# Loading Wk in two pieces and splitting each transposed-tile copy between VectorE and ScalarE at the start of a gated attention-and-MLP kernel

## The chip, the cores and the metric

The kernel runs on one core of a Trainium2 chip. Its time is the device time of one execution in microseconds (us), as the median of several executions. A core has a matrix engine (TensorE, called PE in the profile; PEld is its weight load), a vector engine (VectorE, DVE), an activation engine (ScalarE, ACT), a general engine (GpSimd, POOL) and a queue engine (SyncE, SP). SP, ACT and POOL can issue DMA transfers; what they issue stands in the profile as SPq, ACTq and POOLq. Each engine works through its own list of instructions in order, and waits for others through semaphores.

## The reference

The input x is 2048 rows (tokens) of 512 numbers in bf16. Two blocks work on the same x and are mixed with a gate per row:

```
g   = sigmoid(sum(x * gate_w))                   # one number per row
A:  q, k, v = split(x @ wqkv)                    # 32 heads of 16
    phi(t) = where(t > 0, t + 1, exp(t)) + 1e-6
    kv  = phi(k)^T v per head;  z = sum over rows of phi(k)
    a   = (phi(q) kv) / (phi(q) z + 1e-6) @ wo
B:  h   = layernorm(x);  u = gelu(h^T w1 + b1)   # over the rows: 2048 -> 1792
    b   = (u w2 + b2)^T                          # back to 2048 rows
out = g * a + (1 - g) * b
```

## The kernel before

Rows are cut into 16 tiles of 128 (`NT`), the 512 columns into 4 chunks of 128 (`ND`). The work is written out in one order, and each engine keeps the order in which its own instructions were written. The matrix engine goes through these stages:

1. Six products of constants (`wps`, line 113, called at L201), which need no input.
2. The head: x tiles 0, 1 and 2 are transposed by products with an identity matrix (`pt`), one PSUM bank per tile, and the bank is copied to `xT` in SBUF: by VectorE (L212) for tiles 0 and 2, by ScalarE (L210) for tile 1. Then `k_part` forms K = x Wk for these three tiles (`kacc`, 4 products of 128x128 by 128x512 per tile, one for each chunk of Wk), chunk 0 of all tiles first, then chunk 1, then chunks 2 and 3 tile by tile.
3. A loop over tiles 3 to 15. The transposed x of these tiles comes by transposing DMA loads from SP (L135), the first of which brings tiles 3 and 4. Each turn forms K of tile t, then adds the product of tile t-4 of x and of phi(K) to `gacc` (`g_tile`, which collects x^T phi(K) in four banks). After the loop follow `g_tile` 12 to 15.
4. Q and the first MLP product together (`qacc`, `uacc`), the rest of `uacc`, small products for kv, and last per row tile `aps` and `yps`, mixed by VectorE at L505 and stored.

`phi` of a tile is one exponential on ScalarE (L216) and two operations on VectorE (L217, L220), which write `pk`. VectorE also takes layer-norm statistics (`ln_step`: L240 and L241 per tile). In the head `ln_step(0)` and `ln_step(1)` come before the three `k_phi`; in the loop `ln_step(t - 3)` comes after `k_phi(t)` from t = 5.

At the start SP and ACT issue 7 loads of 128 KB: SP x tile 0 and Wk chunks 0 and 2, ACT x tiles 1 and 2 and Wk chunks 1 and 3. The first transposing load waits for a small VectorE copy (L160) that itself waits for x tile 0. Later SP issues the rest of x, Wq, and w1 in chunks of up to 4 blocks; the first w1 chunk in two transfers, the others in one.

Of the kernel before, what the change touches and what calls it, by code (L numbers as in the profile page):

```python
# [7 lines left out]
ACT = mybir.ActivationFunctionType  # L8
# [7 lines left out]
def kernel(  # L16
# [13 lines left out]
    nc = tc.nc  # L30
# [7 lines left out]
    S, D = X.shape  # L38
    F = B_w1.shape[1]
    NT = S // P  # L40
    ND = D // P
# [13 lines left out]
    wqkv_view = A_wqkv.rearrange("(k p) n -> p k n", p=P)  # L55
# [11 lines left out]
    def keep(shape, dtype, name):  # L67
        return persist.tile(shape, dtype, name=name, tag=name)

    def bank(name, dtype=FP32):  # L70
        return ps.tile([P, SC], dtype, name=name, tag="bank")
# [5 lines left out]
    wk_sb = keep([P, ND, D], BF16, "wk_sb")  # L77
# [34 lines left out]
    def mm(o, lhsT, rhs, start, stop, **kw):  # L112
        nc.tensor.matmul(o, lhsT=lhsT, rhs=rhs, start=start, stop=stop, **kw)  # L113
# [14 lines left out]
    def load_x(q, t0, n):  # L128
        q.dma_start(out=xs[:, t0 : t0 + n, :], in_=x_view[:, t0 : t0 + n, :])

    def load_wk(q, k):
        q.dma_start(out=wk_sb[:, k, :], in_=wqkv_view[:, k, D : 2 * D])

    def load_xT(t0, n):
        nc.sync.dma_start(  # L135
# [1 line left out]
        )  # L137

    load_x(nc.sync, 0, 1)
    load_x(nc.scalar, 1, 1)  # L140
    load_wk(nc.sync, 0)
    load_x(nc.scalar, 2, 1)
    for k, q in ((1, nc.scalar), (2, nc.sync), (3, nc.scalar)):
        load_wk(q, k)
    nc.vector.memset(ones_f[:], 1.0)
    nc.vector.memset(mhalf[:], -0.5)
    nc.vector.memset(Z32[:], 0.0)
# [2 lines left out]
        out=ident[:], in_=ident[:], compare_op=ALU.not_equal, fill=1.0, base=0,  # L150
# [5 lines left out]
        out=maskQ[:], in_=maskH[:].rearrange("p (a m) -> p m a", m=2), op=ALU.max, axis=AX.X  # L156
# [4 lines left out]
        out=xT[:, :, 3 * P : 3 * P + 2],  # L161
        in_=xs[:, 0, 0 : 2 * ND].rearrange("p (k c) -> p k c", k=ND),
# [10 lines left out]
    for c, (j0, nb) in enumerate(w1_chunks):  # L173
        w = wpool.tile([P, NT, FB * P], BF16, name="w1c", tag="wc")
        w1c.append(w)
        for t0 in range(0, NT, 8) if c == 0 else (0,):
            t1 = t0 + 8 if c == 0 else NT
            nc.sync.dma_start(
                out=w[:, t0:t1, : nb * P], in_=w1_view[:, t0:t1, j0 * P : (j0 + nb) * P]
            )  # L180
        if c == 0:
            nc.sync.dma_start(out=wv_sb[:], in_=wqkv_view[:, :, 2 * D : 3 * D])
            nc.sync.dma_start(out=wo_sb[:], in_=wo_view)
# [16 lines left out]
    nc.scalar.activation(out=act_warm[:], in_=ones_f[:], func=ACT.Exp)  # L200
    warm_up(6)  # L201

    def transpose_tile(t, on_act):
        pt = bank("pt")
        for k in range(ND):
            mm(pt[:, k * P : (k + 1) * P], xs[:, t, k * P : (k + 1) * P], ident[:], True, True)
        dst = xT[:, :, t * P : (t + 1) * P]
        src = pt[:].rearrange("p (k s) -> p k s", k=ND)
        if on_act:
            nc.scalar.activation(out=dst, in_=src, func=ACT.Copy)  # L210
        else:
            nc.vector.tensor_copy(out=dst, in_=src)  # L212

    def phi(dst, acc):
        e = work.tile([P, SC], BF16, name="e", tag="e", bufs=6)
        nc.scalar.activation(out=e[:], in_=acc[:], func=ACT.Exp)  # L216
        nc.vector.tensor_scalar(  # L217
            out=e[:], in0=e[:], scalar1=1.0, scalar2=PHI_EPS, op0=ALU.min, op1=ALU.add
        )
        nc.vector.scalar_tensor_tensor(  # L220
            out=dst, in0=acc[:], scalar=0.0, in1=e[:], op0=ALU.max, op1=ALU.add
        )
# [3 lines left out]
    def k_part(t, ks):  # L226
        if t not in kaccs:
            kaccs[t] = bank("kacc")
        for k in ks:
            mm(  # L230
                kaccs[t][:], xT[:, k, t * P : (t + 1) * P], wk_sb[:, k, :],
                k == 0, k == ND - 1,
            )

    def k_phi(t):
        phi(pk[:, t, :], kaccs.pop(t))
# [46 lines left out]
    def ln_step(u):  # L283
        ln_stats(u)
        if u % TPC == TPC - 1:
            ln_rstd(u // TPC)

    HEADS = 3
    transpose_tile(0, False)
    transpose_tile(1, True)  # L290
    transpose_tile(2, False)
    ln_step(0)
    for k in range(2):
        for t in range(HEADS):
            k_part(t, (k,))
    ln_step(1)
    for t in range(HEADS):
        k_part(t, range(2, ND))
        k_phi(t)
    LAG = 4  # L300
    LN_LAG = 3
    APPLY = 9
# [156 lines left out]
    for j in range(NB0, NF):  # L459
        c, jj = divmod(j, FB)  # L460
# [18 lines left out]
        out=gg[:], in0=gth[:], scalar1=0.5, scalar2=0.5, op0=ALU.mult, op1=ALU.add  # L479
    )  # L480
    nc.vector.tensor_scalar(
        out=c1[:], in0=gth[:], scalar1=-0.5, scalar2=0.5, op0=ALU.mult, op1=ALU.add
# [3 lines left out]
    for t in range(NT):  # L486
        c, tl = divmod(t, TPC)
        aps = bank("aps")
        for j in range(ND):
# [3 lines left out]
            out=a_sc[:], in_=aps[:], func=ACT.Identity,  # L493
            scale=gg[:, t : t + 1], bias=c2[:, t : t + 1],
        )
        for c0, W in ((0, D - P), (D - P, P)) if t == NT - 1 else ((0, D),):
            cs = slice(c0, c0 + W)
            yps = bank("yps")
            for f in range(NF):
# [6 lines left out]
                out=ot[:, :W], in0=yps[:, :W], scalar=c1[:, t : t + 1], in1=a_sc[:, cs],  # L506
# [35 lines left out]
```

## Time and profile before

| what | value |
|---|---|
| median of 4 runs | 164.03 us (163.91 to 164.12) |
| profiled execution | 164.07 us, of which the span of the profile is 162.3 us |
| granted TensorE clock | 0.999 |
| PE busy | 158.6 us, 98% of the span |
| DVE busy | 90.0 us, 55%; between 10 and 40 us 26.4 of 30 us |
| ACT busy | 62.8 us, 39% |
| POOL busy | 17.5 us, 11% |
| moved by DMA | 25.18 MB, mean 155 GB/s |

The span runs from the first instruction that the profiler records to the last; some 1.7 us of the profiled execution lie outside it. Times in the profile count from the start of the span. A busy share is an average over stages that have different limits, so the shares alone do not tell what bounds a stage. Ends of matrix products are modelled by the profiler: a product of 512 columns reads as 379 ns, but its neighbours start 216 ns apart.

### The profile page before, as it was taken

Reading aid. Unit: us, or ns where it says so; the run is one execution under the profiler, and the core shown is the slowest. Engines: PE = TensorE matmul, PEld = TensorE weight load, DVE = VectorE, ACT = ScalarE, POOL = GpSimd, SP = SyncE. Lnnn points to the kernel's source line nnn. Section 1 sums busy time; section 2 is a strip of 40 time slices with the busy share of each in tenths; the row PEclk is TensorE's granted clock in tenths of the full one; section 3 lists DMA queues with packets and bytes.
Section 4 is the critical chain, followed back from the end, with each engine's and each line's share of the span. In section 5 each row is a group of like instructions: output and inputs, shape, how many; then the busy total and the mean of one; then the engine's idle time right before and its main releaser. Section 6 shows DMA issues by size and latency. Waiting matters only on the chain.

```text
span 162.3 us, 2189 instructions
## 1 busy us (share of the span) xinstructions
PE 158.6 (98%) x833; PEld 72.5 (45%) x833; DVE 90.0 (55%) x211; ACT 62.8 (39%) x96; POOL 17.5 (11%) x34
## 2 busy tenths in 40 slices
PE   7999999999999999999999999999999999999993
PEld 2444444444444444444444444444444444444452
DVE  1799999957999999519995301255211111111112
ACT  3363386648677483112865113111122222111110
POOL 3000710200110000001504600050000000000000
PEclk9999999999999999999999999999999999999999
DMA  5999999999900007600891699832000001110001
GB/s 153 200 259 259 292 317 346 383 386 386 313 15 0 0 0 227 225 4 0 293 314 44 213 351 284 307 131 78 32 32 32 32 32 41 47 44 33 32 32 32
DMA packets 30569, 25.18 MB, mean 155 GB/s; under 512 B 8480, under 2 KB 29984, under 8 KB 30560
## 3 DMA queue, kind: packets, MB, share of 16 engines
q1 hardware_dynamic: 28256, 21.89, 43.3%
q0 software_dynamic: 1440, 2.38, 5.3%
q10 hardware_dynamic: 864, 0.79, 1.5%
q8 instruction: 6, 0.10, 0.3%
q14 instruction: 3, 0.02, 0.0%
HBM read 21.11 MB, written 2.23 MB: 144 GB/s over the span
## 4 chain that ended last, share of the span: by engine, by line
PE 97%; DVE 1%; issue 0%
PE uacc L113 30%; PE yps L113 30%; PE aps L113 9%; PE qacc L113 9%; PE gacc L113 9%; PE kacc L113 8%; PE wps L113 2%; PE pt L113 1%; PE denps L113 1%; DVE xT L212 0%; PE kvps L113 0%; PE w2ps L113 0%; DVE ot L505 0%; PE pt L335 0%
## 5 line engine op out<-in xcount | busy, mean ns | idle before, releaser
L113 PE MATMUL uacc<-hs,w1c 128*128 128x512 bf16 x224 | 51.3, 379 | 0.0
L113 PE MATMUL yps<-uT,w2c 128*128 128x512 bf16 (+2 forms) x238 | 51.0, 366 | 0.0
L505 DVE SCALAR_TENSOR_TENSOR ot<-yps,c,a_sc 128x512 bf16<-128x512 f32 (+2 forms) x17 | 12.2, 720 | 45.0 <-PE yps L113 44.9
L113 PEld LDWEIGHTS <-w2c 128*128 128x128 bf16 x238 | 22.8, 98 | 25.9
L113 PEld LDWEIGHTS <-w1c 128*128 128x128 bf16 x224 | 21.8, 98 | 26.3 <-issue 0.2
L492 ACT ACTIVATE a_sc<-aps,c,gg 128x512 f32<-128x512 f32 x16 | 12.4, 777 | 46.7 <-PE aps L113 39.9
L329 ACT ACTIVATE uT<-uacc,bcol 128x512 bf16<-128x512 f32 x14 | 9.3, 688 | 21.7 <-PE uacc L113 21.7
L113 PE MATMUL aps<-W2sb,pqT 128*128 128x512 bf16 x64 | 16.4, 379 | 0.0
L113 PE MATMUL qacc<-xT,wq_sb 128*128 128x512 bf16 x64 | 16.4, 379 | 0.0
L113 PE MATMUL kacc<-wk_sb,xT 128*128 128x512 bf16 x64 | 16.1, 380 | 0.1
L113 PE MATMUL gacc<-pk,xs 128*128 128x512 bf16 x64 | 15.8, 379 | 0.0
L256 ACT ACTIVATE hs<-xs,nmr,rstd 128x512 bf16<-128x512 bf16 x16 | 12.8, 806 | 1.8 <-DVE nmr L250 1.8
L216 ACT ACTIVATE e<-qacc 128x512 bf16<-128x512 f32 x16 | 9.6, 597 | 9.2 <-PE qacc L113 9.2
L216 ACT ACTIVATE e<-kacc 128x512 bf16<-128x512 f32 x16 | 9.3, 593 | 9.1 <-PE kacc L113 9.0
L444 POOL DMA_DIRECT2D rex<-rd_dram x16 | 9.4, 598 | 22.5 <-DVE pqT L446 19.2
L220 DVE SCALAR_TENSOR_TENSOR pk<-kacc,e 128x512 bf16<-128x512 f32 x16 | 11.1, 692 | 0.6
L220 DVE SCALAR_TENSOR_TENSOR pqT<-qacc,e 128x512 bf16<-128x512 f32 x16 | 11.1, 692 | 0.6
L113 PEld LDWEIGHTS <-xs 128*128 128x128 bf16 x76 | 7.4, 104 | 8.6 <-DMA xs<-in_A_x_dram 0.9
L240 DVE BATCH_NORM_STATS2 stats<-xs 128x6 f32<-128x512 bf16 x16 | 10.9, 683 | 0.0
L217 DVE TENSOR_SCALAR e<-e 128x512 bf16<-128x512 bf16 x32 | 9.0, 282 | 2.8 <-ACT e L216 2.8
L431 DVE CUSTOM_DVE_ANT_0 junk<-xs,gw_b 128x512 bf16<-128x512 bf16 x16 | 9.8, 685 | 0.0
L113 PEld LDWEIGHTS <-xT 128*128 128x128 bf16 x64 | 6.2, 98 | 7.9 <-DVE xT L212 0.6
(61 smaller groups left out, 73.1 us busy)
## 6 DMA issues: line engine op xcount, KB each, us to landing
w2c<-in_B_w_dram SPq DMA_DIRECT2D x8, 896.0 KB, 6.6
w1c<-in_B_w_dram SPq DMA_DIRECT2D x2, 2048.0 KB, 14.9
w1c<-in_B_w_dram SPq DMA_DIRECT2D x3, 1024.0 KB, 11.8
rex<-rd_dram POOLq DMA_DIRECT2D x16, 128.0 KB, 3.8
out_dram<-ot SPq DMA_DIRECT2D x13, 128.0 KB, 1.7
xs<-in_A_x_dram SPq DMA_DIRECT2D x3, 512.0 KB, 4.2
wq_sb<-in_A_wqkv_dram SPq DMA_DIRECT2D x1, 512.0 KB, 6.1
wv_sb<-in_A_wqkv_dram SPq DMA_DIRECT2D x1, 512.0 KB, 12.1
```

Of the source, the lines that this page charges most:

```text
L113: nc.tensor.matmul(o, lhsT=lhsT, rhs=rhs, start=start, stop=stop, **kw)
L216: nc.scalar.activation(out=e[:], in_=acc[:], func=ACT.Exp)
L217: nc.vector.tensor_scalar(out=e[:], in0=e[:], scalar1=1.0, scalar2=PHI_EPS, op0=ALU.min, op1=ALU.add)
L220: nc.vector.scalar_tensor_tensor(out=dst, in0=acc[:], scalar=0.0, in1=e[:], op0=ALU.max, op1=ALU.add)
L240: nc.vector.bn_stats(out=stats[:], in_=xs[:, t, :])
L256: nc.scalar.activation(out=hs[:, t, :], in_=xs[:, t, :], func=ACT.Identity, scale=rstd[:, t : t + 1], bias=nmr[:, t : t + 1],)
L329: nc.scalar.activation(out=uT[:, j, :], in_=acc[:], func=ACT.Gelu_apprx_tanh, bias=bcol[:, j : j + 1])
L431: nc.vector.tensor_tensor_reduce(out=junk[:], in0=xs[:, t, :], in1=gw_b[:], scale=1.0, scalar=0.0, op0=ALU.mult, op1=ALU.add, accum_out=gp ...
L444: nc.gpsimd.dma_start(out=rex[:], in_=src.unsqueeze(1).to_broadcast([8, HEAD, SC]))
L492: nc.scalar.activation(out=a_sc[:], in_=aps[:], func=ACT.Identity, scale=gg[:, t : t + 1], bias=c2[:, t : t + 1],)
L505: nc.vector.scalar_tensor_tensor(out=ot[:, :W], in0=yps[:, :W], scalar=c1[:, t : t + 1], in1=a_sc[:, cs], op0=ALU.mult, op1=ALU.add,)
```

## The change

Wk is loaded by ACT in two transfers of two chunks (256 KB) each, and all three x tiles by SP. Every transposed tile is copied in two halves: chunks 0 and 1 by VectorE, chunks 2 and 3 by ScalarE. The order on the matrix engine becomes: transposes of tiles 0 and 1, chunks 0 and 1 of K for tiles 0 and 1, transposes of tile 2, then the remaining chunks tile by tile, each tile followed by its `k_phi`. `ln_step(1)` is moved from before the three `k_phi` to after them. The w1 chunks 1 and 2 are loaded in two transfers of 1024 KB each.

```diff
-    def load_wk(q, k):
-        q.dma_start(out=wk_sb[:, k, :], in_=wqkv_view[:, k, D : 2 * D])
+    def load_wk(q, k, n):
+        q.dma_start(out=wk_sb[:, k : k + n, :], in_=wqkv_view[:, k : k + n, D : 2 * D])
...
     load_x(nc.sync, 0, 1)
-    load_x(nc.scalar, 1, 1)
-    load_wk(nc.sync, 0)
-    load_x(nc.scalar, 2, 1)
-    for k, q in ((1, nc.scalar), (2, nc.sync), (3, nc.scalar)):
-        load_wk(q, k)
+    load_wk(nc.scalar, 0, 2)
+    load_x(nc.sync, 1, 1)
+    load_wk(nc.scalar, 2, 2)
+    load_x(nc.sync, 2, 1)
...
-        for t0 in range(0, NT, 8) if c == 0 else (0,):
-            t1 = t0 + 8 if c == 0 else NT
+        for t0 in range(0, NT, 8) if c < 3 else (0,):
+            t1 = t0 + 8 if c < 3 else NT
...
-    def transpose_tile(t, on_act):
+    def transpose_tile(t):
         pt = bank("pt")
         for k in range(ND):
             mm(pt[:, k * P : (k + 1) * P], xs[:, t, k * P : (k + 1) * P], ident[:], True, True)
+        H = ND // 2
+        src = pt[:].rearrange("p (k s) -> p k s", k=ND)
         dst = xT[:, :, t * P : (t + 1) * P]
-        src = pt[:].rearrange("p (k s) -> p k s", k=ND)
-        if on_act:
-            nc.scalar.activation(out=dst, in_=src, func=ACT.Copy)
-        else:
-            nc.vector.tensor_copy(out=dst, in_=src)
+        nc.vector.tensor_copy(out=dst[:, 0:H], in_=src[:, 0:H])
+        nc.scalar.activation(out=dst[:, H:], in_=src[:, H:], func=ACT.Copy)
...
-    transpose_tile(0, False)
-    transpose_tile(1, True)
-    transpose_tile(2, False)
+    transpose_tile(0)
+    transpose_tile(1)
+    for t in range(2):
+        k_part(t, range(2))
+    transpose_tile(2)
     ln_step(0)
-    for k in range(2):
-        for t in range(HEADS):
-            k_part(t, (k,))
+    for t in range(HEADS):
+        k_part(t, range(2 if t < 2 else 0, ND))
+        k_phi(t)
     ln_step(1)
-    for t in range(HEADS):
-        k_part(t, range(2, ND))
-        k_phi(t)
```

## The prediction

> **What bounds the kernel now.** I read the chain of work that ended last, in order of time (columns: start in us, length in us, what). Around the head it reads:
>
> ```profile
> 3.57 1.47 PE pt L113 x12
> 5.05 0.02 issue
> 5.07 0.70 DVE xT L212
> 5.77 0.05 issue
> 5.82 4.06 PE kacc L113 x18
> 9.88 0.86 PE gacc L113 x4
> ```
>
> From 5.82 us on the chain is PE, product after product 0.216 us apart (4.06 / 18 = 0.226 with the first). So an edit in the head is worth what it does to one moment: the start of K of tile 3, after which the list is the same. The head has 12 kacc: two at 4.97 and 5.29, ten from 5.82, so tile 3 starts at 5.82 + 10 x 0.217 = 7.99.
>
> Is PE alone the limit there? The waits up to 8 us (who, for whom, total us, times, longest) and the weight loads at 7.88 (start, length, what, idle before) say no:
>
> ```profile
> PEld L113 <- DVE xT L212: 0.6, 2, 0.4
> PEld L113 <- ACT xT L210: 0.2, 1, 0.2
> PEld L113 <- DMA xT<-in_A_x_dram: 0.2, 1, 0.2
> ```
>
> ```profile
> 7.88 0.21 PEld L113 LDWEIGHTS <-xT 128*128 128x128 bf16 x2 [0.23 <-DMA xT<-in_A_x_dram]
> ```
>
> The first weights of tile 3 were released by the transposing DMA at 7.88, just in time for 7.99. It was issued at 3.75, once x tile 0 had landed, and took 4.1 us. A head that finishes earlier would wait for it: call this floor one.
>
> Floor two is VectorE. Its timeline at the end of the K stage (same columns), and its waits from 8 to 33 us:
>
> ```profile
> 30.96 0.69 DVE L220 SCALAR_TENSOR_TENSOR pk<-kacc,e 128x512 bf16<-128x512 f32 x1
> 31.56 0.69 DVE L240 BATCH_NORM_STATS2 stats<-xs 128x6 f32<-128x512 bf16 x1
> 32.28 0.18 DVE L241 BATCH_NORM_AGGREGATE mv<-stats 128x2 f32<-128x6 f32 x1
> ```
>
> ```profile
> DVE e L217 <- ACT e L216: 0.6, 1, 0.6
> DVE gT L324 <- PE gacc L113: 0.3, 1, 0.3
> ```
>
> Its only two waits are the one that ends at 7.96, before its first operation of phi, and one at 32.80. Between them VectorE is never without work, and the last pk (tile 15) is done at 30.96 + 0.69 = 31.65. `g_tile(15)` starts at 32.16. With about 0.05 for the release that leaves 0.46 us in hand. So work added to VectorE after its first phi, or a first phi that is later, comes out at 32 us as a PE stall once it exceeds 0.46 us.
>
> **The change part by part.** *Loads.* Times to landing, by transfer (columns: tensors, queue, operation, count, size, median us to landing); the rows are SP's three loads and the first transposing load:
>
> ```profile
> xs<-in_A_x_dram SPq DMA_DIRECT2D x1, 128.0 KB, 2.7
> wk_sb<-in_A_wqkv_dram SPq DMA_DIRECT2D x1, 128.0 KB, 2.9
> wk_sb<-in_A_wqkv_dram SPq DMA_DIRECT2D x1, 128.0 KB, 3.7
> xT<-in_A_x_dram SPq DMA_TRANSPOSE x1, 4.1
> ```
>
> Issued at 0.81, 1.26 and 1.73, SP's three land at 3.53, 4.13 and 5.47; ACT's four (0.81, 1.25, 1.74, 2.22) at 3.71, 4.37, 5.66 and 6.07. SP still issues three loads of 128 KB ahead of the transposing one, ACT still moves 512 KB, so I give each transfer the landing of its place: x0 3.53, x1 4.13, x2 5.47, Wk 0-1 4.37, Wk 2-3 6.07. x1 thus comes 0.4 us later than before, and x2 1.1. ACT issues two DMAs instead of four, freeing it some 0.9 us earlier; the table load behind them ended at 3.98 and nothing of ACT's was wanted until 4.64, so this is worth 0. SP's issue of x0 and the transposing load keep their places: floor one stays at 7.99.
>
> *Copies.* A full copy takes 0.692 us on VectorE and 0.597 on ScalarE. L505 shows 351 and 618 ns for 128 and 384 columns, 1.04 ns a column: half a VectorE copy is 0.692 - 256 x 1.04 ns = 0.43. A ScalarE instruction of one column takes 0.204, so its half is about 0.40. Whether both halves run at once no row of before shows, since no bank is read by two engines together. The Trainium skill ("PSUM — Partial Sum Buffer", section "PSUM bank collisions raise a hardware error") says that two engines may not touch one bank in the same partitions at once, reads included. And in the built program each ScalarE half waits for the VectorE half. By the rows alone a tile would be ready 0.43 us after its transposes; by the rule its second half is ready after 0.43 + 0.05 + 0.40 = 0.88, against 0.69 for a whole copy before. I take the rule. Behind the waiting ScalarE half of tile 2 stands the first exponential, and VectorE's first phi waits for that.
>
> *The head.* PE runs at half speed here: `wps` starts are 0.427 apart, transposes 0.107; from 5.82 it is 0.216 per kacc. Step by step:
>
> - Tile 0 transposed 3.57 to 4.00, complete in PSUM 4.18; VectorE half 4.22 to 4.65; weights released at 4.70.
> - Tile 1: x1 at 4.13, transposes 4.17 to 4.60, in PSUM 4.80.
> - kacc of tile 0, chunks 0 and 1: 4.70 and (one at half speed, partly) 5.06.
> - Tile 1: VectorE half 4.84 to 5.27; kacc 5.32 and 5.54, PE free 5.76.
> - Tile 2 (x2 at 5.47 has landed): at full speed 4 x 0.056, in PSUM at 6.15. VectorE half 6.19 to 6.62; ScalarE half from 6.67.
> - Eight kacc from Wk 2-3 at 6.07 (+0.03): 6.10 + 8 x 0.216 = 7.83.
>
> Tile 3 could start at 7.83, but floor one holds it to 7.99: change 0.00. The 0.16 us gained in the head is given back to the transposing DMA.
>
> *VectorE after the head.* ScalarE's half of tile 2 starts at 6.67, and the exponential behind it about 0.28 later (ScalarE's starts overlap: 0.49 apart for 0.597 of length), so 6.95 to 7.55; the first phi on VectorE at 7.59, against 7.96. `ln_step(1)` now comes after it: 0.82 us (6.50 to 7.19 and on, start of one statistic to the next operation). VectorE's run from first phi to last pk was 31.65 - 7.96 = 23.69, and becomes 24.51. Last pk at 7.59 + 24.51 = 32.10, plus 0.05: 32.15 against 32.16. Floor two is met with 0.01 us to spare: the 0.46 in hand is used up, no stall yet. Had `ln_step(1)` stayed hidden in VectorE's wait before the first phi it would cost nothing; here its cover is gone.
>
> *w1 in more transfers.* Chunk 1 landed at 37.6 and is first read at 60.7; chunk 2 at 43.0, read at 76.5. SP's issues end at 37.6 and it then waits for PE. Two more issues behind 23 us of slack: 0.
>
> **Sum.** Both floors sit within 0.01 us of where PE is today. In order of what moves them: x1's landing moves floor two one for one (x1 -> tile 1's half -> tile 2 -> first phi); x0's moves floor one. Each is a floor, so a late one costs and an early one pays only if the other is early as well. I put the likeliest change at +0.07 rather than 0.00 for that reason, the middle of -0.10 to +0.25. The profiled execution is 164.07 (162.3 span and 1.7 around it), 0.04 above the median of 164.03; I add the change to the median: 164.1.
>
> **The rivals.**
> *Slower: the first phi is late.* VectorE has no wait in which to catch up for 24 us, so any delay past 7.60 is paid in full at `g_tile(15)`. The price is x1's landing less 4.14, or the same for whatever holds tile 2. Against the position estimate: Wk 0-1 now runs beside x0 and x1 as one 256 KB transfer. If x1 lands like the third SP load was late (3.7 instead of 2.9 us from issue), at 1.26 + 3.7 = 4.96, the cost is 0.8 us: 164.9; half of that gives 164.4. It decides from an x1 at 4.47 on (0.33 us). The half-speed clock belongs here: the Trainium skill ("TensorE: Matmul & The Clock Gate", section "What's actually happening") says that full speed comes only after a busy window of about 3.4 us, at no fixed moment. The trace has the switch at about 5.0. PE's idle time before 5.0 grows only by some 0.1 to 0.2 us, so by the row the switch stays and costs 0; by the rule, a missed window could leave the two kacc of tile 1, the transposes of tile 2 and two further kacc at half speed: 4 x 0.21 + 0.2 = 1.0, of which 0.2 hides behind waits. I take the row.
>
> *Faster: the transfers are quicker as fewer, larger ones.* If x0 landed 0.35 earlier and x1 followed, both floors and the transposes move by as much: 163.7. For it speaks that PE sits idle for x0 (0.4 us up to 3.57); against it that x0 is still first on SP with another load beside it from ACT.
>
> *The halves do run at once.* Then first phi comes 0.45 earlier and floor two falls away, but floor one stays: change 0.00, the likeliest time again.
>
> **How the numbers follow.** A run of this kernel tells about 0.2% (0.33 us) from no change. Likeliest case, within 0.33 us either way: 0.48, own range 163.85 to 164.35. Late first phi or late clock, 164.37 to 165.0: 0.35. Quicker transfers, 163.4 to 163.7: 0.17. Leaving out about a tenth at each end: 163.6 to 164.8.
>
> **What would show it.** Right: tile 3's weights again released by the transposing DMA near 7.88; the ScalarE half starting after the VectorE half; VectorE's wait before the first phi gone or shorter and first phi near 7.6; last pk near 32.1 and `g_tile(15)` with almost nothing in hand. Wrong: a PE wait for pk at 32 us; x1 landing after 4.47; kacc starts 0.427 apart after 5.1; the transposing load landing before 7.6 with tile 3 following it.

## The result, and the profile after

The changed kernel takes 164.28 us (median of 35 runs, 163.86 to 165.96) against 164.07 us before (55 runs, 163.67 to 164.44): a ratio of 1.0018, with a 95% interval of 1.0010 to 1.0025. That is 0.21 us slower by the medians, 0.16 to 0.41 by the interval: by the medians inside the band called "no change", on its slow side. Two of the 22 executions of the repeat after_again (166.51 and 283.11 us) and one of the kernel before beside it (166.63) were in a slow state, and the ratios leave them out. The profiled execution of the changed kernel took 164.00 us, span 162.29, so it is a quick one; it is 0.06 shorter in span than the one of before, and its total must not be read as the result. Its parts can.

First the head. The chain that ended last, from 0.8 us (start, length, what), in the changed kernel:

```profile
1.26 3.01 DMA xs<-in_A_x_dram
...
4.32 0.41 PE pt L113 x4
4.73 0.02 issue
4.76 0.44 DVE xT L209
5.19 0.05 issue
5.24 0.60 PE kacc L113 x2
5.84 0.32 PE pt L113 x4
6.16 3.45 PE kacc L113 x16
```

By this chain the head now hangs on x tile 1 and on half a copy; x tile 2, which landed at 5.72, then held its own transposes some 0.08 us longer than the products before them. There is no stop at 7.88 any more: the transposing load had landed at 6.96, and K of tile 3 starts at 7.72 instead of 7.99. The rows of x tile 0 and of the transposing load (last number: us from issue to landing) say why:

```profile
xs<-in_A_x_dram SPq DMA_DIRECT2D x1, 128.0 KB, 2.2
xT<-in_A_x_dram SPq DMA_TRANSPOSE x1, 3.7
```

x tile 0 took 2.2 us instead of 2.7, so the transposing load was issued at 3.27 instead of 3.75, and it took 3.7 us instead of 4.1. The transposes of tile 0 moved up less, from 3.57 to 3.36: until then PE is busy with its products of constants.

The halves, on VectorE and ScalarE (start, length, what, idle before and what ended it):

```profile
4.03 0.42 DVE L209 CAST xT<-pt 128x256 bf16<-128x256 f32 x1 [0.79 <-PE pt L113]
```

```profile
4.48 0.38 ACT L210 ACTIVATE xT<-pt 128x256 bf16<-128x256 f32 x1 [1.16 <-DVE xT L209]
```

ScalarE waits for VectorE, as the built program has it, and starts 0.03 after it ends. The bank is read by one engine after the other, in 0.42 and 0.38 us.

Then the end of the K stage: on VectorE (first and last operation of phi), the chain there, and the weight loads of the last product before `g_tile(15)` and of its first:

```profile
7.56 0.29 DVE L215 TENSOR_SCALAR e<-e 128x512 bf16<-128x512 bf16 x1
...
31.36 0.69 DVE L218 SCALAR_TENSOR_TENSOR pk<-kacc,e 128x512 bf16<-128x512 f32 x1
```

```profile
29.90 2.16 PE gacc L113 x10
32.06 0.04 issue
32.10 1.02 PE gacc L113 x4
```

```profile
31.68 0.10 PEld L113 LDWEIGHTS <-xs 128*128 128x128 bf16 x1
32.10 0.10 PEld L113 LDWEIGHTS <-xs 128*128 128x128 bf16 x1 [0.32 <-issue]
```

VectorE's first phi is at 7.56, the last pk done at 31.36 + 0.69 = 32.05, and `g_tile(15)` starts at 32.10, 0.05 later. The product before it started at 31.68, 0.42 earlier, where neighbours are 0.216 apart: PE waited 0.21 us. What the head had gained, 0.27, is given back here but for 0.06.

In eleven of the fourteen profiles, those of the experiments below included, one sum holds, with the two numbers read from each trace: span = start of K of tile 3 + wait at `g_tile(15)` + 154.36.

| kernel | K of tile 3 | wait | span | span less both |
|---|---|---|---|---|
| before | 7.99 | 0.00 | 162.35 | 154.36 |
| before_again | 8.05 | 0.00 | 162.41 | 154.36 |
| before_again_2 | 8.14 | 0.00 | 162.50 | 154.37 |
| changed | 7.72 | 0.21 | 162.29 | 154.36 |
| after_again | 8.56 | 0.21 | 163.14 | 154.36 |
| gap_fill | 7.75 | 0.21 | 162.32 | 154.36 |
| whole_copies | 7.94 | 0.13 | 162.42 | 154.35 |
| before_stats_late | 7.79 | 0.29 | 162.44 | 154.36 |
| stats_fill | 8.37 | 0.00 | 162.73 | 154.36 |
| stats_fill_2 | 7.83 | 0.00 | 162.19 | 154.36 |
| x_first | 7.94 | 0.00 | 162.32 | 154.38 |

Three further profiles have 0.07 to 0.36 us more outside these parts (x_pair, w1_whole, old_loads); in them too PE's last product starts where the sum puts it, and the rest lies after it.

### The profile page after: what moved, and what is told of

It reads as the page before. It is cut to its first block, busy times and chain, and to the rows that moved or that the text cites. A ratio compares the mean times of both kernels' runs of the same rounds, so it can differ in the third digit from the quotient of the medians.

```text
span 162.3 us, 2191 instructions
## 1 busy us (share of the span) xinstructions
PE 158.2 (97%) x833; PEld 72.1 (44%) x833; DVE 90.2 (56%) x212; ACT 63.1 (39%) x98; POOL 17.5 (11%) x34
## 4 chain that ended last, share of the span: by engine, by line
PE 95%; DMA 2%; DVE 0%; SPq 0%; issue 0%
PE uacc L113 30%; PE yps L113 30%; PE gacc L113 9%; PE qacc L113 9%; PE aps L113 9%; PE kacc L113 8%; DMA xs<-in_A_x_dram 2%; PE denps L113 1%; PE pt L113 0%; PE kvps L113 0%; DVE xT L209 0%; SPq L129 0%; PE w2ps L113 0%; DVE ot L502 0%; PE pt L332 0%
## 5 line engine op out<-in xcount | busy, mean ns | idle before, releaser
L279 DVE TENSOR_TENSOR zacc<-zacc,pk 128x512 f32<-128x512 f32 x14 | 9.6, 685 | 0.2
```

Of the source, the lines that this page charges most:

```text
L279: nc.vector.tensor_tensor(out=zacc[:], in0=first, in1=pk[:, t, :], op=ALU.add)
```

## The experiments

Two theories stood once the profile above was known. F: VectorE is a second floor, and the moved statistics use up what was in hand. L: late x tiles stall PE in the head, and VectorE does not matter. The kernels were timed in three groups, each beside the kernel before: 164.16 us in the first group (after_again, before_stats_late, stats_fill, whole_copies), 164.07 in the second (old_loads, w1_whole, gap_fill, x_first) and in the third.

**after_again**: the changed kernel, no edit.

> The changed kernel once more, for a second profile and its time beside the others. Theory F (VectorE is a second floor: no idle time from its first phi to the last pk, and the moved statistics of tile 1 use up what was in hand): 0.1 to 0.3 us slower than before; the profile again shows the product of tile 15 of gacc held until the last pk, and the kernel's shift equals (first phi - 7.60). Theory L (late loads of x tiles 1 and 2 stall PE in the head itself, VectorE is irrelevant): the same time, but K of tile 3 starts as much later as the time is longer and nothing is held at 32 us.

Measured: 164.34 us (22 runs), ratio 1.0005 (0.9990 to 1.0021), too wide to add to the main result. Its profile is of an execution of 164.87 us, and shows two things at once. The wait at `g_tile(15)` is there again, 0.21. And K of tile 3 starts at 8.56, 0.84 later than in the first profile. The kacc rows up to 6.5 us (count: length in ns least/median/most, first and last start), first profile, then this one:

```profile
L113 PE MATMUL kacc<-wk_sb,xT x7: 379/379/389, 4.6 to 6.4; 128*128 128x512 bf16 x7
```

```profile
L113 PE MATMUL kacc<-wk_sb,xT x4: 541/634/634, 5.0 to 6.2; 128*128 128x512 bf16 x4
```

Four products here started 0.427 us apart, at half speed. The profile's own row of the granted clock does not show it: it reads 1.00 from 4.9 to 6.6 us in both profiles, so the speed is read from the starts. The switch to full speed came at about 6.5 us, against some moment between 3.8 and 4.3 in the first profile and 5.0 in that of before. x tile 1 landed 0.23 later as well (4.51 against 4.28), which leaves some 0.6 of the 0.84 to the clock. So both theories had a part: L's shift of the head is real, but its main cause is the clock; F's wait is on top of it.

**before_stats_late**: the statistics alone, in the kernel before.

```diff
             k_part(t, (k,))
-    ln_step(1)
     for t in range(HEADS):
         k_part(t, range(2, ND))
         k_phi(t)
+    ln_step(1)
```

> The kernel before with one edit: the statistics of tile 1 stand after the three phi of the head instead of ahead of them; loads, copies and the order on PE as before. Theory F: 0.82 us more after the first phi on VectorE against 0.46 in hand, so the last pk at about 32.47, the product of tile 15 held to 32.52, and 0.36 us slower than before. Theory L: no load is touched, 0.0.

Measured: 164.43 us, ratio 1.0023 (1.0015 to 1.0031), that is 0.25 to 0.5 us slower; 0.36 was expected. Nothing but the place of two VectorE instructions differs. The chain of this kernel names VectorE where that of before has PE alone:

```profile
31.52 0.70 DVE pk L220
32.22 0.04 issue
32.26 1.02 PE gacc L113 x4
```

In this profile the first phi is at 7.72, not 7.96, because full speed came at 3.6; the last pk is then at 32.21 and the wait 0.29. Its run from first phi to `g_tile(15)` is 24.54, as the changed kernel's is (32.10 - 7.56). No load and no product was moved, so L is out as the whole story.

**stats_fill** and **stats_fill_2**: the statistics moved into VectorE's wait, in the changed kernel.

```diff
+    ln_step(0)
     transpose_tile(2)
-    ln_step(0)
+    ln_step(1)
...
         k_phi(t)
-    ln_step(1)
```

> The changed kernel with the statistics of tile 0 written before the transposes of tile 2 and those of tile 1 right after them, ahead of the three phi, so that they fill VectorE's wait of 1.0 us for tile 2. Theory F: the last pk comes 0.8 us earlier (about 31.25 in the profile), no PE wait at 32 us, and the time falls 0.2 to 0.3 us under the changed kernel's, to about 0.1 below before. Theory L: the wait at 32 us was not the cost, and the time stays at the changed kernel's, 0.2 above before.

> The changed kernel with the statistics ahead of the phi once more, for a tighter time and another profile. Theory F: about 0.2 us under the changed kernel, so 0.0 from before within 0.1; no wait at 32 us; the span is the start of K of tile 3 plus 154.36.

Measured: 164.17 us, ratio 1.0003 (0.9991 to 1.0015), and 164.10 us, 1.0000 (0.9990 to 1.0010). The wait is gone in both profiles; in the second, PE's chain runs through:

```profile
29.79 3.24 PE gacc L113 x15
33.03 0.65 PE uacc L113 x3
```

```profile
30.66 0.69 DVE L218 SCALAR_TENSOR_TENSOR pk<-kacc,e 128x512 bf16<-128x512 f32 x1
```

The last pk is at 31.35, and `g_tile(15)` starts at 32.00, 0.65 later and without a wait. With the edit the changed kernel is level with before; neither interval reaches the 1.0018 of the main result. Against after_again, timed beside the first of the two, the intervals are too wide to tell them apart. The 0.1 below before that was expected did not come: one of the two profiles again has a late switch (about 6.4 us; K of tile 3 at 8.37).

**whole_copies**: the halves undone (`on_act` for tile 1 alone, as before), the rest as changed.

```diff
...
-        nc.vector.tensor_copy(out=dst[:, 0:H], in_=src[:, 0:H])
-        nc.scalar.activation(out=dst[:, H:], in_=src[:, H:], func=ACT.Copy)
+        if on_act:
+            nc.scalar.activation(out=dst, in_=src, func=ACT.Copy)
+        else:
+            nc.vector.tensor_copy(out=dst, in_=src)
...
```

> The changed kernel with whole copies again (tiles 0 and 2 by VectorE, tile 1 by ScalarE), the rest as changed. K of tile 0 waits 0.2 us longer, but x tile 2 still holds the next transposes; VectorE's first phi 0.06 later (7.62 against 7.56). Theory F: 0.0 to 0.1 us slower than the changed kernel. If the halves were what costs (a ScalarE half that waits for VectorE and delays the first exponential): up to 0.2 us faster than it.

Measured: 164.31 us, ratio 1.0011 (1.0003 to 1.0020); not told apart from the changed kernel. In its profile K of tile 3 is at 7.94 and the wait 0.13. `g_tile(15)` starts at 32.24, against 32.10 to 32.22 in the three early-switch profiles with halves (changed, gap_fill, w1_whole): by the profiles the halves are worth about 0.1 us, by the times up to about 0.3 us either way stays open.

**old_loads**: the seven loads of before under the new order.

```diff
-    load_wk(nc.scalar, 0, 2)
-    load_x(nc.sync, 1, 1)
-    load_wk(nc.scalar, 2, 2)
-    load_x(nc.sync, 2, 1)
+    load_x(nc.scalar, 1, 1)
+    load_wk(nc.sync, 0, 1)
+    load_x(nc.scalar, 2, 1)
+    for k, q in ((1, nc.scalar), (2, nc.sync), (3, nc.scalar)):
+        load_wk(q, k, 1)
```

> The changed kernel with the seven loads of 128 KB of before (x tiles 1 and 2 and Wk 1 and 3 on ACT, x tile 0 and Wk 0 and 2 on SP), copies, order and statistics as changed. x tile 0 lands at 3.5 again instead of 3.0 to 3.1, the first transposing load at 7.8 instead of 7.0 to 7.5, x tile 2 at 4.4 instead of 5.7, Wk 1 at 5.7 instead of 3.9. By the steps: K of tile 0 chunk 1 waits for Wk 1 to 5.7, three more kacc and the transposes of tile 2 end at 6.5, K of tile 3 at 8.2: 0.2 to 0.5 us slower than the changed kernel, so the new loads are a gain in themselves. If the loads are not what matters (theory F alone): as the changed kernel, 0.0 to 0.1.

Measured: 165.26 us, ratio 1.0072 (1.0045 to 1.0098): some 0.9 us slower than the changed kernel, twice the most that was expected. PE's first product of K started at 4.50, the second waited for Wk 1 until 5.99, and K of tile 3 started at 8.59. Its wait in the profile from 4 to 8 us (who, for whom, us in total, times, longest):

```profile
PE kacc L113 <- DMA wk_sb<-in_A_wqkv_dram: 1.1, 1, 1.1
```

The new order needs the new loads: chunk 1 of Wk is its second product.

**w1_whole**: w1 chunks 1 and 2 in one transfer each.

```diff
-        for t0 in range(0, NT, 8) if c < 3 else (0,):
-            t1 = t0 + 8 if c < 3 else NT
+        for t0 in range(0, NT, 8) if c == 0 else (0,):
+            t1 = t0 + 8 if c == 0 else NT
```

> The changed kernel with w1 chunks 1 and 2 in one transfer each, as before. All theories: 0.0, since the chunks land 23 us ahead of their use.

Measured: 164.42 us, ratio 1.0022 (1.0014 to 1.0030), as the changed kernel. The split is worth nothing that can be seen.

**gap_fill**: products of constants where PE waits for x tile 1.

```diff
     transpose_tile(0)
+    warm_up(1)
+    warm_up(1, SC // 2)
     transpose_tile(1)
```

> The changed kernel with one and a half products of constants (one of 512 and one of 256 columns) put on PE between the transposes of tile 0 and of tile 1, where it waits 0.5 to 0.8 us for x tile 1. The profiles so far have PE going from half to full speed at 3.6, 3.7, 4.2, 5.0, 6.4 and 6.6 us. Theory C1 (the idle time that the change opens before tile 1 delays full speed): the late switches become rare and the median falls 0.1 to 0.3 us, to about before. Theory C2 (the moment lies anywhere in 3.2 to 6.6 us, by chance, whatever the gap): the same median as the changed kernel's within 0.1, executions still spread over 163.9 to 164.9; K of tile 3 near 7.7 with an early switch and near 8.5 with a late one. Either way the product of tile 15 waits 0.2 us for the last pk.

Measured: 164.25 us, ratio 1.0011 (0.9998 to 1.0024). Three of 14 executions lay above 164.6, against 11 of 55 of the unedited changed kernel (35, and 20 of after_again). That the idle time delays the clock is neither shown nor excluded.

**before_again** and **before_again_2**: two more profiles of the kernel before.

> The kernel before, a second profile. Theory C2 (the switch to full speed falls anywhere in 3.2 to 6.6 us): another moment than 5.0; with a switch before 5.8, K of tile 3 at 7.8 to 8.0; with one at 6.5, at about 8.3, since fewer products stand between 5.8 and the switch than in the changed kernel (8.56). The span is the start of K of tile 3 plus 154.36.

> The kernel before, a third profile, as the second: K of tile 3 at 7.8 to 8.0 with an early switch to full speed, 8.1 to 8.3 with one after 6.0; the span is that plus 154.36.

Measured: 164.15 and 164.24 us. The switch came at about 5.9 us (the product of K that started at 5.28 still ran its 631 ns of half speed, the next 470) and at about 5.1; K of tile 3 at 8.05 and 8.14. The sum with 154.36 held. A switch after 6 us was not met, so its price in this kernel is not known.

**x_first** and **x_pair**: two attempts to beat both kernels. Both transpose the three tiles first and put the statistics ahead of the phi. They differ in the loads: x_first

```diff
     load_x(nc.sync, 0, 1)
+    load_x(nc.scalar, 1, 1)
+    load_x(nc.sync, 2, 1)
     load_wk(nc.scalar, 0, 2)
-    load_x(nc.sync, 1, 1)
     load_wk(nc.scalar, 2, 2)
-    load_x(nc.sync, 2, 1)
...
-    for t in range(2):
-        k_part(t, range(2))
     transpose_tile(2)
     ln_step(0)
+    ln_step(1)
     for t in range(HEADS):
-        k_part(t, range(2 if t < 2 else 0, ND))
+        k_part(t, range(2))
+    for t in range(HEADS):
+        k_part(t, range(2, ND))
         k_phi(t)
-    ln_step(1)
```

> Meant to beat both: statistics of tiles 0 and 1 ahead of the phi, all three x tiles first (0 and 2 from SP, 1 from ACT), then Wk in two loads from ACT, and the three transposes first on PE. x tile 1 lands at 3.7, x tile 2 near 4.2, Wk 0-1 near 4.9, Wk 2-3 near 5.9; K of tile 3 at 7.8 to 8.0, held by the transposing load as before; first phi near 7.5 with no statistics after it, last pk at about 31.2 and no wait at 32 us. Theory F: 0.0 to 0.15 us faster than before, 0.2 to 0.35 faster than the changed kernel. If late x tiles and not VectorE were the cost, as much again from the earlier landing: 0.3 faster than before.

and x_pair, against x_first

```diff
-    load_x(nc.scalar, 1, 1)
-    load_x(nc.sync, 2, 1)
-    load_wk(nc.scalar, 0, 2)
+    load_x(nc.scalar, 1, 2)
+    load_wk(nc.sync, 0, 2)
```

> Meant to beat both. SP loads x tile 0 and then Wk chunks 0 and 1 in one transfer, ACT loads x tiles 1 and 2 in one transfer of 256 KB and then Wk chunks 2 and 3; transposes of the three tiles first, chunks 0 and 1 of K for all three, then chunks 2 and 3 with phi; statistics of tiles 0 and 1 ahead of the phi. In every profile where ACT begins with a 256 KB transfer x tile 0 lands at 3.0 to 3.2 instead of 3.5 and the first transposing load at 7.0 to 7.5. So: x tiles 1 and 2 near 3.9, Wk 0-1 near 4.6, Wk 2-3 near 5.4; K of tile 3 at 7.5 to 7.8 with an early switch to full speed and 8.0 to 8.3 with a late one (before: 7.99 with a switch at 5.0); last pk near 31, no wait at 32 us. Time 0.2 to 0.4 us under before. If x tile 0 lands at 3.5 all the same: 0.0 to 0.1 under before.

Measured: x_first 164.07 us, ratio 0.9993 (0.9984 to 1.0002); x_pair 164.13 us, 0.9999 (0.9983 to 1.0016). Neither beats the kernel before beyond its interval. In x_first the transposing load landed at 7.89 and K of tile 3 began at 7.94, the floor of before. x_pair has two kinds of execution, seven at 163.62 to 163.92 and seven at 164.33 to 164.81. Its profile is of the second kind: Wk 0-1 landed at 5.79, not near 4.6, and PE stood idle for it. What the quick ones do was not seen.

## Why the prediction was right, and where its steps were not

The forecast was 164.1, range 163.6 to 164.8, with "no change within 0.33 us" likeliest and the slower side ahead of the faster; the medians differ by 0.21. The number came in, and the floor that decides was named. But of its own signs of being wrong the first profile shows one, a PE wait for pk at 32 us, and half of another: the transposing load landed before 7.6, though tile 3 followed PE and not the load.

*Floor two held, in its length to a few hundredths.* Expected: first phi 7.59, last pk 32.10, `g_tile(15)` at 32.15. Measured: 7.56, 32.05, 32.10. The run from first phi, with the moved statistics in it, was put at 24.51 plus 0.05 and measures 24.54. That the first phi itself came within 0.03 was luck: x tiles 1 and 2 landed 0.15 and 0.25 late, the switch to full speed came some 0.7 us or more early, and these misses cancelled; in after_again, with a late switch, it came at 8.40. That the statistics are what makes it bind is shown from both sides: put late in the kernel before they cost 0.25 to 0.5 us, taken early in the changed kernel they give the wait back.

*The halves held.* 0.42 and 0.38 against 0.43 and 0.40, one after the other. The program sets this order, and it fits the rule of the Trainium skill ("PSUM — Partial Sum Buffer", section "PSUM bank collisions raise a hardware error") that two engines may not be at one bank in the same partitions at once; no run here lets them try. The first exponential started at 6.93 against 6.95.

*Floor one failed.* The step "SP's issue of x0 and the transposing load keep their places: floor one stays at 7.99" gave each transfer the landing of its place in the queue. x tile 0 landed at 3.05, not 3.53, and the transposing load at 6.96, not 7.84. So the gain of the head was not given back to that load. PE reached K of tile 3 at 7.72 (7.83 was expected of PE itself), and for that reason met floor two, which would have had 0.01 to spare. The rival "faster" took the whole of an earlier x tile 0 for PE, with 0.4 us of idle time before 3.57. The starts give 0.21: the last product of constants starts at 2.93 and is done 0.427 later, at 3.36, and there the transposes begin in the changed kernel, though x tile 0 is in at 3.05.

*Two landings were off the other way.* x tile 2 at 5.72 instead of 5.47, x tile 1 at 4.28 instead of 4.13; Wk 0-1 and 2-3 at 3.89 and 5.03 instead of 4.37 and 6.07. What held the transposes of tile 2 (5.76) was x tile 2, by a little, not the kacc before them (done at 5.68).

*Why the loss is steady.* In the changed kernel's order both the first phi and K of tile 3 hang on tile 2's transposes: first phi comes 0.16 before K of tile 3 in the profiles of the changed kernel, after_again, gap_fill and w1_whole alike, whatever the head's delay. From K of tile 3 PE would reach `g_tile(15)` in 24.17 (32.16 - 7.99), VectorE lets it go 24.54 after the first phi: 24.54 - 0.16 - 24.17 = 0.21. That is the wait of 0.20 to 0.21 in all four. The head's start, by itself, was on average no gain: 7.72, 7.75, 7.84 and 8.56 in these four profiles, 7.99 to 8.14 in three of before. The difference of the medians, 0.21, equals that wait: taken back through the sum, K of tile 3 would start at about 8.00 in the median of either kernel. That is an estimate from the two medians and the 1.7 us outside the span, not a measurement.

*The clock was the right rival with the wrong row.* I took the switch at 5.0 as fixed. It is not: it lay between about 3.6 and 6.5 in the profiles here. The Trainium skill ("TensorE: Matmul & The Clock Gate", section "What's actually happening") has a free-running window of about 3.4 us, which allows for this; the 500 ns either way that it gives for the switch is less than the 2.9 us found here, and the measurement decides. The changed order has its products in just that stretch (from 4.56 on, where before most of them start at 5.82), so a late switch costs it more. K of tile 3 starts 3.36 to 3.52 us after x tile 1 lands in four profiles of this order with a switch before 4.7 (changed, gap_fill, w1_whole, stats_fill_2), and 4.06 and 4.11 after it in the two with a switch at 6.4 to 6.5 (after_again, stats_fill): an estimate of some 0.6 us, where the prediction's rival had 0.8. How often that happens, and how much of the difference of medians it carries beside the 0.21, the runs do not settle.

## What to carry to other kernels

An engine that is not the bound may still have no wait in which to catch up: look at its waits over the whole stage, find the last of its results that the bound engine needs, and count how much is in hand there before moving work from its idle time into its busy time. When a head is made quicker, follow both branches that leave it to where they meet again; what was gained on one may be lost on the other 24 us later. Judge a change in the first microseconds by several profiles, since the clock may be another in each.

## What the runs showed of the hardware that was not expected

- With a first transfer of 256 KB on ACT, in place of 128 KB, SP's first transfer tended to land sooner: x tile 0 landed at 3.00 to 3.25 us in the eight profiles with 256 KB first, at 3.20 to 3.53 in the six with 128 KB first. A later start of ACT's packets does not explain it. In the packet records SP's first packet starts at 1.83 to 1.85 us in all fourteen, ACT's at 2.20 to 2.51 in the eight and at 1.96 to 2.34 in the six, and of the six the one with the earliest ACT packet (1.96, before_again_2) has the earliest x tile 0 (3.20). The cause is open.
- The switch to full speed came anywhere from about 3.6 to 6.5 us with the same six products of constants starting at 0.84 us. In the clock records of the ten traces that have one, full speed then lasts 157.01 or 160.43 us, two lengths 3.42 apart, though the head and the span differ from run to run.
